# Agent attention and a mixture of experts on one core: the score products of a unit kept together on the tensor engine, and the first keys taken two units at a time

## The chip, the cores and the metric

The kernel runs on one core of one Trainium2 chip, in one launch. The metric is device time in microseconds (us). A core has five engines with an instruction queue each: PE (TensorE, matrix products; PEld are its weight loads), DVE (VectorE), ACT (ScalarE), POOL (GpSimd) and SP (SyncE, which here issues the loads). PE writes to PSUM, eight banks, from which DVE and ACT fetch. An f32 product shows as two records in the trace, an f16 product as one.

## The reference, cut to what matters

There are 4 batches of 11456 rows of 128 numbers (q, k, v), 49 agents, and 8 experts with a hidden layer of 1024.

```python
def sm(a, b):                       # softmax of scaled products
    s = scale * (a @ b.transpose(0, 2, 1))
    e = np.exp(s - s.max(-1, keepdims=True))
    return e / (e.sum(-1, keepdims=True) + 1e-09)

agent_v = sm(agents, k) @ v         # weighted values of each agent
x = sm(q, agents) @ agent_v         # every query's row
# expert per row: argmax of the cosine of x with 8 embeddings, and its gate
h = np.maximum(x[mask] @ w1[e], 0.0)
out[mask] = gate_w[mask, None] * (h @ w2[e])
```

All is f32. Rows of one batch go mostly to one expert; the few others ("strays") are answered apart.

## The kernel before, in words

A batch is cut into 12 units: 11 of 8 columns of 128 rows, and a small one of 2 columns of 96. For a unit of keys or of queries, `pe_T` (L412) turns the rows on PE, eight transposes into two PSUM banks (L419), and two copies bring them to SBUF: the first half on ACT (L424), the second on DVE (L422), or on ACT too where `two` is false. Then `scores` (L427) makes the products with the 49 agents (L432). Each product there takes 64 columns of the array: a column of 128 rows is two products, for the two halves of the array, and a whole unit is 16 products, 32 records. `k1_f32` (L435) does this for keys and keeps the scores and a running maximum; `q_unit` (L885) does it for queries and goes on to the softmax, to `rtp` (L935, the routing products) and to the rows `tt` that the expert's products read. In batches 2 and 3 every other unit of keys goes through `k1_pairs` (L456) instead, in f16 with DMA transposes. `k2_unit` (L503) takes the exponentials of the keys' scores and makes the weighted values (L523), again with half of the array: 8 products, 16 records a unit. The expert's products (`ffn_mm1` L1192, L1193; `ffn_mm2` L1216 to L1230) and the products that show which rows the shortcut holds for (`proved`, L1045, L1048) use the whole array.

Every unit is a Python generator. `run_step` lets all live generators go on by turns, and the order in which they write their instructions down is the program's order. Tile's scheduler then orders each engine's queue: of the instructions whose inputs and buffers are ready it puts the one that stands first in the program; inside `tc.high_priority(n)` an instruction counts as if it stood n instructions earlier, and `tc.issue_after(i)` (here `in_place` and `behind`) puts it behind instruction i on its engine. The first-layer products of the expert are asked for with 200. SP's queue is kept in the order of the program.

The program has two parts. `first` (L1493) takes batch 0's keys and values, the first four units of queries, and six units of batch 1's keys. From the point where `ffn_at[0]` is set, a loop over ticks runs the expert's products of the batches one after the other, and beside them the later keys, values and queries.

Buffers that matter: three for turned data (`xT`, XB = 3), four PSUM banks for transposes and first-layer products (`ps_h`), two for the expert's results (`ps_y`), and two for scores, weighted values, routing and the small products (`ps_s`). Ten buffers hold loaded units (LB = 10); a load waits until the tenth unit before it is used up. The weights of a batch's expert are loaded by `load_expert` (L872, L873), once `pick_expert` has found it from the weighted values.

Of the kernel before, what the change touches and what calls it, by code (L numbers as in the profile page):

```python
# [29 lines left out]
def kernel(ctx: ExitStack, tc: tile.TileContext, q, k, v, agents, emb, tau, w1, w2, out):  # L30
    nc = tc.nc
    pe, dve, act, pool, sp = nc.tensor, nc.vector, nc.scalar, nc.gpsimd, nc.sync

    B, N, C = q.shape
    A = agents.shape[1]
# [19 lines left out]
    LO = 64  # L55
    FP = 2 * P
    RW = E + 1 + A
    W = D + 1
    UT = 2
    UJ = UT * TJ  # L60
    NU = (J + UJ - 1) // UJ + 1
# [27 lines left out]
    def pss(name):  # L89
        return ps_s.tile([P, 512], F32, name=name, tag="s")  # L90
# [35 lines left out]
    ffn_at = [None]  # L126
# [3 lines left out]
    def used(*unit):  # L130

        ring[slot[unit]][1] = now[0]
# [40 lines left out]
    ident = cst.tile([P, P], F32, name="ident")  # L173
# [205 lines left out]
    def in_place(last):  # L379

        return tc.issue_after(last[-1].ins) if last else nullcontext()
# [23 lines left out]
    def run_max(kb, spv, p, n):  # L405
# [3 lines left out]
        else:  # L409
            dve.tensor_tensor(out=mr, in0=spv, in1=mr, op=ALU.max)  # L410

    def pe_T(src, p, n, two=True):  # L412

        xT = wk.tile([P, 2 * UJ, P], F16, name="fT", tag="xT", bufs=XB).rearrange("k c p -> k (c p)").bitcast(F32)
        for c0 in range(0, n, TJ):
            m = min(TJ, n - c0)
            tp = psh("fTp")
            for c in range(m):
                pe.transpose(out=tp[:, c * p : (c + 1) * p], in_=src[:p, c0 + c, :], identity=ident[:p, :p])  # L419
            dst = xT[:, c0 * p : (c0 + m) * p]  # L420
            if c0 and two:
                dve.tensor_copy(dst, tp[:, : m * p])  # L422
            else:
                act.copy(dst, tp[:, : m * p])  # L424
        return xT

    def scores(s, xT, b, p, n):  # L427

        for c in range(n):
            for h in range(0, p, LO):  # L430
                w = min(LO, p - h)
                pe.matmul(out=s[h : h + w, c * A : (c + 1) * A], lhsT=xT[:, c * p + h : c * p + h + w], rhs=aT_all[:, b, :],  # L432
                          start=True, stop=True, skip_group_check=True)

    def k1_f32(b, u):  # L435

        kb = blk_of(b, u)
        p, n = ushape(u)
        yield from here(("k", b, u))
        i = yield from take(x_slots)  # L440
        kb.at[u] = yield from take(s_slots)
        with in_place(warmed) if b + u == 0 else behind(asked["k", b, u]):
            kT = pe_T(units["k", b, u], p, n, b != 1 or u >= NEXT)
        used("k", b, u)
        yield 2
        s = pss("sp")
        scores(s, kT, b, p, n)
        give(x_slots, i)
        st = wk.tile([P, UJ, A], F32, name="s_u", tag="s_u", bufs=NU)[:p, :n]
        spv = s[:p, : n * A].rearrange("p (c a) -> p c a", a=A)  # L450
        act.copy(st, spv)
        run_max(kb, spv, p, n)
        kb.s[u] = st
        kb.k1 += 1
# [48 lines left out]
    def k2_unit(b, u, eng, g):  # L503

        kb = blk_of(b, u)
        p, n = ushape(u)
        while ("v", b, u) not in units:
            yield 1
        src = units["v", b, u]

        i = yield from take(d_slots)
        de = kds[i % len(kds)].rearrange("p c a -> p (c a)")
        d = de[:p, : n * A].rearrange("p (c a) -> p c a", a=A)
        eng.tensor_tensor(out=d, in0=kb.s[u], in1=kb.m[:p].unsqueeze(1).broadcast_to([p, n, A]), op=ALU.subtract)
        give(s_slots, kb.at[u])
        yield g[0]
        act.activation(d, d, AF.Exp, scale=SCALE)
        yield g[1]
        avp = pss("avp")

        for c in range(n):
            hs = slice(LO * (c % 2), LO * (c % 2) + LO)
            pe.matmul(out=avp[hs, :W], lhsT=de[:p, c * A : c * A + LO], rhs=src[:p, c, :], start=(c < 2), stop=(c >= n - 2),  # L523
                      skip_group_check=True)
        used("v", b, u)
        give(d_slots, i)
        if kb.k2 == 0:
            kb.x = sm.tile([P, W], F32, name="avx", tag="avx", bufs=2)
            dve.tensor_copy(kb.x, avp[:, :W])
        else:  # L530
            dve.tensor_tensor(out=kb.x, in0=avp[:, :W], in1=kb.x, op=ALU.add)
        kb.k2 += 1
# [352 lines left out]
    def q_unit(b, u, g):  # L885
        bt = batches[b]
        p, n = ushape(u)
        yield from here(("q", b, u))
        tt_of[b, u] = yield from take(t_slots, len(checks(b, u)) + sum(unit_of(t)[0] == u for t in range(NT)))
        f32 = b == 0 and u < LEAD  # L890
        i = yield from take(x_slots)
        with in_place(p_last) if p_last else behind(asked["q", b, u]):
            xT = pe_T(units["q", b, u], p, n, b < B - 1)
        used("q", b, u)
        yield g[0]
        s = pss("sp")
        scores(s, xT, b, p, n)
        give(x_slots, i)
        spv = s[:p, : n * A].rearrange("p (c a) -> p c a", a=A)
        mx = sm.tile([P, UJ], F32, name="qmx", tag="qmx")[:p, :n]  # L900
        dve.tensor_reduce(out=mx, in_=spv, axis=AX.X, op=ALU.max)
        ie = yield from take(qe_slots)
        e = wk.tile([P, UJ, A], F32, name="qe", tag="qe", bufs=LEAD)[:p, :n]
        dve.tensor_tensor(out=e, in0=spv, in1=mx.unsqueeze(2).broadcast_to([p, n, A]), op=ALU.subtract)
        yield g[1]
        act.activation(e, e, AF.Exp, scale=SCALE)  # L906
        yield g[2]
        i = yield from take(e_slots)
        e2 = e16[i % len(e16)]
        hi = e2[:p, :n, :A]  # L910
        i_ = act.copy(hi, e)  # L911
        if not ffn_at[0]:
            q_last[:] = [i_]
        (dve if f32 else pool).tensor_tensor(out=e2[:p, :n, LO : LO + A], in0=e, in1=hi, op=ALU.subtract)  # L914
        tt = wk.tile([P, UJ * P], F16, name="tt", tag="tt", bufs=TB)
        if f32:
            tp = psh("tp").bitcast(F16)
            for c in range(n):
                pe.transpose(out=tp[:, c * p : (c + 1) * p], in_=e2[:p, c, :], identity=ident16[:p, :p])
            act.copy(tt[:, : n * p], tp[:, : n * p])  # L920
        else:
            if ffn_at[0]:
                yield 8
            sp.dma_start_transpose(out=tt[:, : n * p].rearrange("k (c p) -> k c p", p=p),
                                   in_=e2[:p, :n, :].rearrange("p c k -> p (c k)"))
        give(e_slots, i)
        yield g[3]
        tts[b, u] = tt
        while not hasattr(bt, "r_hi"):
            yield 1  # L930
        s = (pss if ffn_at[0] else psh)("rtp")
        with in_place(y_last):
            for c in range(n):
                o = s[:p, c * RW : (c + 1) * RW]
                pe.matmul(out=o, lhsT=tt[:, c * p : (c + 1) * p], rhs=bt.r_hi, start=True, stop=False)  # L935
                pe.matmul(out=o, lhsT=tt[:, c * p : (c + 1) * p], rhs=bt.r_lo, start=False, stop=True)
        gi = group_of[u]
        us = groups[gi]
        if (b, gi) not in rtgs:
            rtgs[b, gi] = wk.tile([P, GC, E + 1], F32, name="rtg", tag="rtg", bufs=4)  # L940
        if not hasattr(bt, "qq"):
            bt.qq = sm.tile([P, 2, NCOL], F32, name="qq", tag="qq")
        rtg, qq = rtgs[b, gi], bt.qq
        c0 = ucol(u) - ucol(us[0])
        cs = slice(c0, c0 + n)
        if p < P:
            pmem(rtg[p:, cs], 1.0)
            pmem(qq[p:, :, ucol(u) : ucol(u) + n], 1.0)
        sv = s[:p, : n * RW].rearrange("p (c w) -> p c w", w=RW)
        rt = wk.tile([P, 2, UJ, A], F32, name="rt", tag="rt", bufs=1)[:p, :, :n]  # L950
        act.copy(rtg[:p, cs], sv[:, :, : E + 1])
        pool.tensor_tensor(out=rt[:, 1], in0=e, in1=e, op=ALU.mult)  # L952
        dve.tensor_tensor(out=rt[:, 0], in0=sv[:, :, E + 1 :], in1=e, op=ALU.mult)  # L953
        give(qe_slots, ie)
        yield 1
        pool.tensor_tensor(out=rt[:, :, :, : A // 2], in0=rt[:, :, :, : A // 2], in1=rt[:, :, :, A // 2 + 1 :], op=ALU.add)  # L956
        yield g[4]
        dve.tensor_reduce(out=qq[:p, :, ucol(u) : ucol(u) + n], in_=rt[:, :, :, : A // 2 + 1], axis=AX.X, op=ALU.add)
        routed[b, gi] = routed.get((b, gi), 0) + 1
        if routed[b, gi] == len(us):  # L960
            spawn(route_group(b, gi, sum(ushape(x)[1] for x in us)), 1, half=True)
# [750 lines left out]
```

## Time and profile before

| | |
|---|---|
| median of 3 runs | 716.54 us (716.29 to 717.41) |
| profiled execution | 717.31 us, span 715.4 us |
| PE busy | 660.7 us (92%) |
| DVE busy | 539.6 us (75%) |
| ACT busy | 459.8 us (64%) |
| POOL busy | 343.8 us (48%) |
| scores L432, PE | 98.7 us busy in 2496 records |
| mean granted clock of TensorE | 0.979 |

PE is the fullest engine. The groups' mean durations are latencies: products overlap, so what one costs PE is read from the starts of it and of the next. The page's slices show PE at nine or ten tenths nearly everywhere, with less near the start and at the very end.

### The profile page before, as it was taken

What the parts mean: (1) busy time and instruction counts of PE and PEld (TensorE: products, weight loads), DVE (VectorE), ACT (ScalarE), POOL (GpSimd) and SP (SyncE); (2) the same over time, 40 slices, a digit from 0 to 9 for tenths busy, and PEclk for the clock granted to TensorE, in tenths of its full rate; (3) what the DMA queues carried; (4) which work ended last, traced back from release to release, by engine and by line L of the source; (5) the groups of instructions that cost most, each with busy time, mean ns of one, the idle gap of its engine ahead of it and who ended that gap; (6) DMA issues with size and microseconds to landing.
All of it is one profiled execution on the core that took longest, in us unless ns stands there. A gap on an engine that the chain in (4) does not pass through costs nothing. (4 is left out here: it accounts for less than half of the span.)

```text
span 715.4 us, 23225 instructions
## 1 busy us (share of the span) xinstructions
PE 660.7 (92%) x9279; PEld 559.4 (78%) x9279; DVE 539.6 (75%) x1475; ACT 459.8 (64%) x1129; POOL 343.8 (48%) x579
## 2 busy tenths in 40 slices
PE   9987899999999899799999899999999898889996
PEld 7885777888888677678888787778888686777876
DVE  5768866787667998865767789975657699986983
ACT  4438646668678746666679854855577844976632
POOL 6004311395416555656524673764544663886500
PEclk9998899999999999999999999999999999999999
DMA  8995328699778349987969165994567242325232
GB/s 340 280 346 191 90 65 205 161 219 276 187 175 220 102 96 211 288 230 186 245 166 233 52 166 116 272 261 107 184 180 189 60 110 64 78 47 152 71 131 78
DMA packets 152823, 122.11 MB, mean 171 GB/s; under 512 B 72563, under 2 KB 128967, under 8 KB 152715
## 3 DMA queue, kind: packets, MB, share of 16 engines
q1 hardware_dynamic: 139275, 96.92, 52.9%
q10 hardware_dynamic: 13120, 23.47, 9.8%
q8 instruction: 73, 1.20, 0.7%
q0 software_dynamic: 320, 0.24, 0.1%
q14 instruction: 35, 0.29, 0.1%
HBM read 80.26 MB, written 23.79 MB: 145 GB/s over the span
## 5 line engine op out<-in xcount | busy, mean ns | idle before, releaser
L1054 ACT ACTIVATE vp<-vp 128x512 f32<-128x512 f32 x180 | 106.1, 589 | 18.7 <-PE vp L1045 15.8
L1201 ACT ACTIVATE hh<-hp 128x512 f16<-128x512 f32 (+1 forms) x124 | 72.9, 592 | 53.0 <-PE hp L1193 32.4
L1202 DVE SCALAR_TENSOR_TENSOR hh<-hp,hh 128x512 f16<-128x512 f32 (+1 forms) x124 | 84.0, 678 | 28.0 <-ACT hh L1201 27.4
L432 PE MATMUL sp<-aT_all,fT 128*64 128x49 f32 x2496 | 98.7, 225 | 3.6 <-DVE esa L1012 2.8
L432 PEld LDWEIGHTS sp<-aT_all,fT 128*64 128x64 f32 x2496 | 84.7, 137 | 21.8 <-issue 10.6
L1228 PE MATMUL yp<-w2p,hh 128*128 128x128 f16 (+1 forms) x492 | 92.6, 220 | 3.0 <-DVE w2p L842 2.3
L1229 PE MATMUL yp<-w2p,hh 128*128 128x128 f16 (+1 forms) x492 | 92.7, 220 | 0.0
L1230 PE MATMUL yp<-w2p,hh 128*128 128x128 f16 (+1 forms) x492 | 91.8, 220 | 0.0
L1045 PE MATMUL vp<-vm,tt 128*128 128x256 f16 x360 | 71.0, 274 | 3.1 <-DVE vmin L1051 1.4
L1192 PE MATMUL hp<-tt,gh 128*128 128x512 f16 (+1 forms) x184 | 69.3, 377 | 4.0 <-DVE fT L422 1.6
L424 ACT COPY fT<-fTp 128x512 f32<-128x512 f32 (+1 forms) x101 | 55.6, 564 | 24.7 <-PE fTp L419 16.8
L1244 DVE TENSOR_TENSOR ot<-yp,gs 128x512 f32<-128x512 f32 (+1 forms) x92 | 61.1, 670 | 12.0 <-PE yp L1230 5.9
L1193 PE MATMUL hp<-tt,gl 128*128 128x512 f16 (+1 forms) x184 | 69.0, 375 | 0.0
L995 POOL TENSOR_TENSOR nrm<-qq,half 128x16 f32<-128x16 f32 (+2 forms) x28 | 68.5, 2447 | 0.3
L914 POOL TENSOR_TENSOR e<-qe,e 128x392 f16<-128x392 f32 (+1 forms) x44 | 40.2, 914 | 56.9 <-ACT e L911 55.7
L1216 PE MATMUL yp<-lin,tt 128*128 128x128 f16 x720 | 63.6, 220 | 3.5 <-DVE ot L1244 3.5
L1225 PE MATMUL yp<-w2f,hh 128*128 128x128 f32 (+1 forms) x456 | 65.6, 281 | 0.0
L956 POOL TENSOR_TENSOR rt<-rt 128x384 f32<-128x384 f32 (+1 forms) x48 | 42.4, 884 | 44.7 <-DVE rt L953 26.3
L1225 PEld LDWEIGHTS yp<-w2f,hh 128*128 128x128 f32 (+1 forms) x456 | 58.4, 193 | 2.2
L1216 PEld LDWEIGHTS <-tt 128*128 128x128 f16 x720 | 49.8, 99 | 12.0 <-issue 4.5
L419 PE MATMUL fTp<-ident,qt 128*128 128x128 f32 x360 | 55.4, 281 | 2.5 <-DVE fT L422 1.1
L952 POOL TENSOR_TENSOR rt<-qe 128x392 f32<-128x392 f32 (+1 forms) x48 | 38.9, 810 | 37.2 <-ACT qe L906 24.4
(374 smaller groups left out, 1744.3 us busy)
## 6 DMA issues: line engine op xcount, KB each, us to landing
kt<-in_k_dram SPq DMA_DIRECT2D x44, 512.0 KB, 6.3
vt<-in_v_dram SPq DMA_DIRECT2D x44, 512.0 KB, 6.2
qt<-in_q_dram SPq DMA_DIRECT2D x44, 512.0 KB, 5.4
out_dram<-ot ACTq DMA_DIRECT2D x88, 256.0 KB, 3.3
w1s<-in_moe_w_dram SPq DMA_DIRECT2D x9, 512.0 KB, 3.8
w2s<-in_moe_w_dram SPq DMA_DIRECT2D x9, 512.0 KB, 5.9
tt<-e SPq DMA_TRANSPOSE x44, 3.9
kt<-in_k_dram SPq DMA_DIRECT2D x4, 96.0 KB, 3.8
```

Of the source, the lines that this page charges most:

```text
L432: pe.matmul(out=s[h : h + w, c * A : (c + 1) * A], lhsT=xT[:, c * p + h : c * p + h + w], rhs=aT_all[:, b, :], start=True, stop=True, skip ...
L1045: pe.matmul(out=z[:p, i * FP : (i + 1) * FP], lhsT=tt[:, c * p : (c + 1) * p], rhs=bt.vm[:, LO:], start=True, stop=True)
L1054: act.activation(z[:p], z[:p], AF.Relu, scale=-1.0, accum_out=bt.vsum[:p, at : at + 1])
L1192: pe.matmul(out=hp[:, :m], lhsT=bt.gh[:, fs], rhs=tt, start=True, stop=False)
L1193: pe.matmul(out=hp[:, :m], lhsT=bt.gl[:, fs], rhs=tt, start=False, stop=True)
L1201: h_last[:] = [act.activation(hh[:, :m], hp[:, :m], AF.Relu)]
L1202: dve.scalar_tensor_tensor(out=hl[:, :m], in0=hp[:, :m], scalar=0.0, in1=hh[:, :m], op0=ALU.max, op1=ALU.subtract)
L1216: pe.matmul(out=yp[:p, c, :], lhsT=tc_, rhs=bt.lin[:, h], start=(c == 0 and h == 0), stop=False, skip_group_check=True)
L1225: y_last[:] = [pe.matmul(out=y, lhsT=hh[:, cs], rhs=bt.w2f[:, f], start=False, stop=last, skip_group_check=True)]
L1228: pe.matmul(out=y, lhsT=hh[:, cs], rhs=wh, start=False, stop=False, skip_group_check=True)
L1229: pe.matmul(out=y, lhsT=hh[:, cs], rhs=wl, start=False, stop=False, skip_group_check=True)
L1230: y_last[:] = [pe.matmul(out=y, lhsT=hl[:, cs], rhs=wh, start=False, stop=last, skip_group_check=True)]
```

## The change

Scores and weighted values that are written down after `ffn_at[0]` is set come into `tc.high_priority(300)`; before that point nothing changes for them, with one exception. For batch 0's keys, a unit of odd number (1, 3, 5, 7, 9) writes its scores only when the unit two further on has been turned, and puts them behind the last transpose of that unit on PE. `pe_T` notes its last transpose in `turn` for this.

```diff
+    turn, k_turned = [], {}
+    def whole():
+        return tc.high_priority(300) if ffn_at[0] else nullcontext()
...
     def pe_T(src, p, n, two=True):
...
-                pe.transpose(out=tp[:, c * p : (c + 1) * p], in_=src[:p, c0 + c, :], identity=ident[:p, :p])
+                turn[:] = [pe.transpose(out=tp[:, c * p : (c + 1) * p], in_=src[:p, c0 + c, :], identity=ident[:p, :p])]
...
     def k1_f32(b, u):
...
+        k_turned[b, u] = turn[0]
         yield 2
+        two = b == 0 and u % 2 and u + 2 < NU
+        while two and (b, u + 2) not in k_turned:
+            yield 1
         s = pss("sp")
-        scores(s, kT, b, p, n)
+        with in_place([k_turned[b, u + 2]]) if two else whole():
+            scores(s, kT, b, p, n)
...
     def k2_unit(b, u, eng, g):
...
-        for c in range(n):
-            hs = slice(LO * (c % 2), LO * (c % 2) + LO)
-            pe.matmul(out=avp[hs, :W], lhsT=de[:p, c * A : c * A + LO], rhs=src[:p, c, :], start=(c < 2), stop=(c >= n - 2),
-                      skip_group_check=True)
+        with whole():
+            for c in range(n):
+                hs = slice(LO * (c % 2), LO * (c % 2) + LO)
+                pe.matmul(out=avp[hs, :W], lhsT=de[:p, c * A : c * A + LO], rhs=src[:p, c, :], start=(c < 2), stop=(c >= n - 2),
+                          skip_group_check=True)
...
     def q_unit(b, u, g):
...
-        scores(s, xT, b, p, n)
+        with whole():
+            scores(s, xT, b, p, n)
```

## Rows read from the trace of the kernel before

**Rows 1.** Windows: length, busy us of each engine, then PEclk, DMA share, GB/s
```profile
8.00:29.00 21.00, 21.00 (x397) 18.66 (x395) 13.32 (x25) 10.04 (x21) 6.15 (x33) 1.00 1.08 341
...
44.00:53.00 9.00, 6.98 (x78) 6.74 (x78) 5.04 (x21) 2.08 (x6) 0.00 (x0) 0.81 0.92 344
...
103.00:650.00 547.00, 513.51 (x7257) 434.57 (x7256) 419.92 (x1125) 374.16 (x940) 296.03 (x464) 0.99 0.66 168
```

**Rows 2.** Timeline of PE: start us, length us, line, operation, tiles, count
```profile
355.12 0.38 PE L1192 MATMUL hp<-tt,gh 128*128 128x512 f16 x1
355.33 0.38 PE L1193 MATMUL hp<-tt,gl 128*128 128x512 f16 x1
355.64 1.14 PE L432 MATMUL sp<-aT_all,fT 128*64 128x49 f32 x32
356.71 0.28 PE L1045 MATMUL vp<-vm,tt 128*128 128x256 f16 x1
```

**Rows 3.** Timeline of PE, two units of scores in one run
```profile
231.85 2.07 PE L432 MATMUL sp<-aT_all,fT 128*64 128x49 f32 x64
233.86 0.39 PE L1045 MATMUL vp<-vm,tt 128*128 128x256 f16 x2
```

**Rows 4.** Timeline of PE, 114 to 123 us, scores in ten runs
```profile
114.26 0.56 PE L432 MATMUL sp<-aT_all,fT 128*64 128x49 f32 x12
114.75 0.39 PE L1045 MATMUL vp<-vm,tt 128*128 128x256 f16 x2
115.07 0.32 PE L432 MATMUL sp<-aT_all,fT 128*64 128x49 f32 x2
115.32 0.66 PE L419 MATMUL fTp<-ident,kt 128*128 128x128 f32 x4
...
121.69 1.13 PE L432 MATMUL sp<-aT_all,fT 128*64 128x49 f32 x30
122.75 1.09 PE L419 MATMUL fTp<-ident,kt 128*128 128x128 f32 x8
```

**Rows 5.** Timeline of PE, other units in several runs, the first and the last
```profile
107.05 0.67 PE L432 MATMUL sp<-aT_all,fT 128*64 128x49 f32 x16
...
150.75 0.44 PE L523 MATMUL avp<-vt,kd 128*64 128x129 f32 x4
...
537.70 0.32 PE L432 MATMUL sp<-aT_all,fT 128*64 128x49 f32 x2
...
538.49 1.13 PE L432 MATMUL sp<-aT_all,fT 128*64 128x49 f32 x30
```

**Rows 6.** Timeline of ACT and DVE, copies of turned halves, two units
```profile
107.52 0.57 ACT L424 COPY fT<-fTp 128x512 f32<-128x512 f32 x1
...
108.35 0.69 DVE L422 COPY fT<-fTp 128x512 f32<-128x512 f32 x1 [1.59 <-PE fTp L419]
...
550.31 0.61 ACT L424 COPY fT<-fTp 128x512 f32<-128x512 f32 x1
...
551.69 0.57 ACT L424 COPY fT<-fTp 128x512 f32<-128x512 f32 x1
```

**Rows 7.** Groups by line: busy us, mean ns, idle us before and its releasers
```profile
L432 PE MATMUL sp<-aT_all,fT 128*64 128x49 f32 x2496 | 98.7, 225 | 3.6 <-DVE esa L1012 2.8 <-DVE w2p L842 0.5 <-ACT kd L517 0.3
...
L935 PE MATMUL rtp<-r_hi,tt 128*128 128x58 f16 x352 | 25.9, 190 | 5.1 <-DMA tt<-e 3.0 <-DVE w2p L842 0.9 <-DVE ee L1401 0.6
```

**Rows 8.** Timeline of PE, first keys and first products on the expert's weights
```profile
8.92 1.09 PE L419 MATMUL fTp<-ident,kt 128*128 128x128 f32 x8
9.94 1.14 PE L432 MATMUL sp<-aT_all,fT 128*64 128x49 f32 x32
...
52.82 1.96 PE L698 MATMUL gp<-avT,w1s 128*128 128x49 f32 x16 [0.45 <-DVE qmx L901]
```

**Rows 9.** Landing of two k loads issued 41.1 and 42.0, then w1s issued 48.7
```profile
DMA to landing us min/median/max: 9.0/9.1/9.3
...
DMA to landing us min/median/max: 4.0/4.0/4.0
```

## The prediction

> **What bounds the kernel now.** I read the windows of equal work first, then PE's timeline, then the copies that feed the products, then the landings of the loads. In the long stretch in which the expert's products run, 103 to 650 us, PE is busy 513.5 of 547 us (94%), at the full granted clock (0.99, the 2.4 GHz level) [rows 1]. DVE has 420 and ACT 374 of the same 547. So 94% of a PE microsecond saved there is a microsecond of the end, as long as PE's input is ready. Before 53 us it is otherwise: PE is full from 8 to 29 us, but the DMA engines are full as well (share 1.08, and 0.92 from 44 to 53, where PE is at 0.81) [rows 1].
>
> **The price that the change is after.** Scores (L432) and weighted values (L523) use the array as two halves of 64 columns; all other products use it whole. PE's timeline shows what each change between the two costs. The product L1193 takes 0.21 us to its successor when that is an ordinary one (355.12 to 355.33 is the same form), but the scores behind it start 0.31 later: 0.09 to go in [rows 2]. A whole unit of scores (32 records, two to a product) lasts 1.07 us to the next product [rows 2], two units back to back 2.01 [rows 3]: 0.94 for 32 more, 0.0294 each, so 1.07 holds 0.94 of work and 0.13 to come out. One break inside a unit costs 0.09 + 0.13, with rounding 0.23 us. Checked on a part: 12 records should take 0.13 + 0.35 = 0.48, and take 0.49 (114.26 to 114.75); 2 records should take 0.19 and take 0.25, since the cut goes through a pair of halves [rows 4].
>
> The Trainium skill, "TensorEngine Tiling (Array Packing)", section "Key Properties", says that a change of tiling mode drains TensorE, and "TensorE: Matmul & The Clock Gate", section "Single matmul latency", puts the fixed part of a single product at 166 ns at the full clock; two drains would make a break 0.33 us (an estimate from that page), and the 18 breaks below 6.0 us instead of 5.0. The 0.23 of this trace decides.
>
> **How many breaks there are.** From 114.26 to 122.75 three units of scores lie in ten runs, of 12, 2, 8, 20, 2, 10, 2, 8, 2 and 30 records, with transposes and vp, hp and yp products between them (the first two and the last run in [rows 4]). Start to next start the ten runs take 4.48 us, where three whole units take 3.21; with seven further entries at 0.094 that is 1.93 us for seven breaks, 0.28 each. In the whole stretch I count 18 breaks in 12 units: two at 107, these seven, one each at 325, 372, 465 and 537, two at 484, and three in weighted values, which are cut at 150, 180 and 183 us (first and last in [rows 5]). 18 x 0.28 = 5.0 us. A cut at 92 us is in a unit that is written down before the new priority holds, and stays.
>
> **What the priority removes.** A scores or weighted-values product of this stretch is placed as if it stood 300 instructions earlier, ahead of the first-layer products at 200. What cuts the units now is ready work that stands earlier in the program, so all 18 can go: 5.0 x 0.94 = 4.7 us.
>
> **What it adds.** Three things, none shown by this trace.
> (a) The scores no longer queue behind older work, so they come when their first half is ready. A unit's transposed data comes by two copies. In 33 of its 55 whole units the second ends over 0.6 us after the first, more than the 0.56 that half a unit takes (0.09 + 0.47); the first and the last of the 33 are in [rows 6] (0.57 after 107.52, then 0.69 after 108.35; 550.92, then 552.26). Now the scores usually start 1 to 4 us after both, and this lag is hidden. If they start at once, PE, which has other work ready, puts it between the halves: a new break of 0.23. Bounds: none, and 33 x 0.23 x 0.94 = 7.2 us. The row nearest to this is the crowded stretch at 105 to 128 us, where six units follow their copies within about 1 us: one of them has a first run of 16 records, exactly half [rows 5]. One in six of 62 units is 10: 10 x 0.23 x 0.94 = 2.2 us.
> (b) With no slack behind its copy, a unit can make PE itself wait, and everything behind it in PE's queue waits too (yp and hp, then ACT and DVE). Scores idle PE for 3.6 us over 84 units now; rtp products, which do come close behind their input, idle it for 5.1 over 44 [rows 7]. At rtp's 0.116 a unit against 0.043 it would be 62 x 0.073 = 4.5 us; without rtp's waits for a DMA (3.0), which scores don't have, 0.3. I take 0.3; below nothing is possible by up to 1, if earlier scores shorten rtp's own waits.
> (c) Nine pairs of units now share one entry and one exit by chance ([rows 3] is one). Priority can part them (9 x 0.23 = 2.1 us at worst) or make as many new ones. I take 0.
>
> **First keys two at a time.** From 8 us on transposes and scores alternate, unit by unit, with no idle PE [rows 1, 8]. Five pairs of units now share a change: 5 x 0.23 = 1.2 us of PE. The transposes that are moved ahead need the next load 2 us earlier at most once (the fourth unit, at 9.9), and the buffers of the turned data just suffice, three for three. What is late next is the first expert: its weights are issued at 48.7 us and land 4.0 us later, and the products on them start at 52.82 [rows 8, 9]. The k loads ahead of them on SP's queue were issued at 41.1 and 42.0 and needed 9.0 and 9.3 us, so they land at 50.1 and 51.3 [rows 9], and 0.5 MB at the 344 GB/s of these microseconds [rows 1] takes 1.5 us: the weights land right behind them however early they are asked for. So I cost the saving at 0, hidden by the DMA stream; the other bound is the whole 1.2 us, if the weights kept their 4.0 us and came earlier.
>
> The Trainium skill, "DMA: Bandwidth & Descriptors", section "Queues, rings and completion order", says that each DMA engine takes the descriptors of one ring in order. By that the weights can't pass the keys and the gain is 0; without it, 1.2 us. The spacing of the landings here agrees with the rule.
>
> **Sum.** -4.7 + 2.2 + 0.3 + 0 = -2.2 us. The profiled execution took 717.31 us (715.4 of span and 1.9 around it), so 715.1 for it; the median of the runs shown is 0.77 lower, and 716.54 - 2.2 = 714.3 is the forecast. About 0.2% of this time, 1.4 us, can be told from no change.
>
> **Rivals.**
> Torn at the halves (slower). The mechanism is (a) alone: every one of the 33 units with a late second copy is cut there. 7.2 + 0.3 - 4.7 = +2.8: 719.3 us. It decides from about 22 units on (4.7 / 0.217), where it eats the whole gain. For it: the lag is there in 33 of 55 units. Against: a unit also needs a score bank, of which there are two, and while it waits for one its second half lands.
> A draw. Some 18 to 22 units are cut at the half, about as many breaks as go: 716.5 us. For it: the same rows; this is only the middle of (a).
> All of it. No new cuts, and the first keys' 1.2 us come through: -4.7 - 1.2 = -5.9, 710.6 us. For it: PE is the bound for 547 us. Against: rows 6 and 9.
> It doesn't do what it says. What cuts the units is that their input isn't ready, not older work; then priority changes only the weighted values (3 x 0.25 x 0.94 = 0.7): 715.8 us. Against: the cuts at 114 to 122 fall after 12, 2 and 8 records, not at halves.
>
> **How the numbers follow.** Forecast 0.36, of which 0.27 is beyond 1.4 us and 0.09 within; its own range is 712.5 to 716. All of it 0.17, faster. A draw 0.20, of which 0.18 same and 0.02 slower. Torn 0.21, slower. Doesn't do it 0.06, same. Together faster 0.44, same 0.33, slower 0.23. The range 710.8 to 719.3 leaves out half of "all of it" and less than half of "torn".
>
> **What would show it.** In PE's timeline, the runs of L432's line of under 32 records: with the change, cuts after 2, 8, 10 or 12 records should be gone, and what is left should be 16 and 16. Ten units cut so bears out the forecast, over 22 the slower rival, none the best case. Weighted values should all be runs of 16 or 32. The idle time before the scores should stay under 5 us. Scores of the first keys should show as runs of 64, and the first products on the expert's weights should still start at 52.5 to 53 us; if they start near 51.6, the DMA was not the cover I take it for. The prediction is wrong if PE's idle time in 103 to 650 us moves by more than 3 us, since then the order of the work, and not the price of the breaks, sets the result.

## The result, and the profile after

The changed kernel takes 709.96 us (median of 6 runs, 708.62 to 713.9), the kernel before 717.93 beside it (6 runs). The ratio is 0.9898, 95% interval 0.9874 to 0.9922: 8.0 us less, where 2.2 less was forecast. 709.96 lies below the range (710.8 to 719.3). The profiled execution of the changed kernel, from which all its rows come, is the longest of its six: 713.9 us, span 711.9, so its rows show 3.4 of the 8.0 us. The ratios here leave out slow runs (over 1.5% above the fastest of their kernel: two, of the changed kernel at 190), and are not quotients of the medians shown, from which they differ by up to 0.5%.

Lines are numbered anew: scores are L438 now, transposes L425, weighted values L535, the expert's products L1205 to L1243. In the kernels of the experiments they shift by a few more; the tile names stay.

The windows of the changed kernel, with two short ones added (columns as in [rows 1]):

```profile
8.00:29.00 21.00, 20.95 (x430) 19.47 (x429) 14.41 (x26) 11.33 (x24) 6.25 (x34) 1.00 1.08 341
44.00:53.00 9.00, 6.08 (x72) 5.81 (x71) 5.35 (x20) 2.74 (x8) 0.14 (x1) 0.81 1.00 360
103.00:650.00 547.00, 521.97 (x7409) 447.17 (x7407) 420.71 (x1145) 378.20 (x963) 301.22 (x480) 0.98 0.68 172
160.00:166.00 6.00, 4.08 (x66) 3.29 (x65) 3.29 (x7) 2.69 (x6) 5.83 (x10) 1.00 1.12 237
167.00:173.00 6.00, 5.41 (x41) 4.40 (x42) 2.79 (x6) 2.34 (x6) 0.48 (x2) 0.50 0.85 238
```

From 103 to 650 us PE does 7409 products where it did 7257 [rows 1]. Its idle time there is 547 less 521.97, 25.0 us; it was 33.5. The prediction had said that it is wrong if this moves by more than 3 us. At the same time the clock is worse: from 160 to 166 us it is full, from 167 to 173 at 0.50, the 1.2 GHz level.

PE's timeline of the changed kernel: the first keys, the first products on the expert's weights, a stretch that answers to [rows 4], and a long wait:

```profile
9.02 1.97 PE L425 MATMUL fTp<-ident,kt 128*128 128x128 f32 x16
10.92 2.07 PE L438 MATMUL sp<-aT_all,fT 128*64 128x49 f32 x64
12.92 1.97 PE L425 MATMUL fTp<-ident,kt 128*128 128x128 f32 x16
...
53.70 1.70 PE L710 MATMUL gp<-avT,w1s 128*128 128x49 f32 x7 [2.29 <-DMA w1s<-in_moe_w_dram]
...
109.69 0.67 PE L438 MATMUL sp<-aT_all,fT 128*64 128x49 f32 x16
110.29 0.66 PE L425 MATMUL fTp<-ident,kt 128*128 128x128 f32 x4
110.88 0.67 PE L438 MATMUL sp<-aT_all,fT 128*64 128x49 f32 x16
...
163.40 0.67 PE L438 MATMUL sp<-aT_all,fT 128*64 128x49 f32 x16
167.59 1.01 PE L1229 MATMUL yp<-lin,tt 128*128 128x128 f16 x8 [3.51 <-DVE ot L1257]
```

The first keys are as built: 64 records of scores behind 16 transposes, 3.90 us for two units. The cuts after 2, 8, 10 and 12 records [rows 4] are gone. Six units of scores are still cut, every one 16 and 16, as at 109.69 and 110.88; weighted values are never cut. In the whole program the half-array products lie in 112 runs, 134 before.

What the scores wait for, and the two groups that changed most:

```profile
L438 PE MATMUL sp<-aT_all,fT 128*64 128x49 f32 x2496 | 97.8, 226 | 3.9 <-DVE esa L1025 2.6 <-DVE m_run L410 0.7 <-DVE rt L966 0.6
...
L1229 PE MATMUL yp<-lin,tt 128*128 128x128 f16 x720 | 64.1, 223 | 10.7 <-DVE ot L1257 10.7
...
L948 PE MATMUL rtp<-r_hi,tt 128*128 128x58 f16 x360 | 28.6, 192 | 4.5 <-DMA tt<-e 3.9 <-DVE qe L917 0.5
```

Scores idle PE for 3.9 us (3.6 in [rows 7]). The new waits are elsewhere: yp waits 10.7 us for DVE to empty its bank, 3.5 before. In the kernel before PE's longest waits were (us in all, times, longest):

```profile
PE tp L919 <- DVE e L914: 4.8, 2, 3.3
PE yp L1216 <- DVE ot L1244: 3.5, 4, 1.4
PE sqT L1286 <- DMA xq<-in_q_dram,ix: 3.2, 2, 1.8
```

The longest wait of yp in the changed kernel, in the timeline of all engines:

```profile
165.96 0.23 POOL L1029 TENSOR_TENSOR el<-el,la 128x16 f32<-128x16 f32 x1
...
166.22 0.25 DVE L1032 RECIPROCAL gs<-el 128x16 f32<-128x16 f32 x1 [0.85 <-POOL el L1029]
...
166.50 0.31 ACT L1036 ACTIVATE gs<-gs,iall 128x16 f32<-128x16 f32 x1
...
166.84 1.29 DVE L1257 TENSOR_TENSOR ot<-yp,gs 128x512 f32<-128x512 f32 x2 [0.38 <-ACT gs L1036]
```

The gate of the rows comes from POOL by way of DVE and ACT, and only then does DVE take the result out of its bank. POOL is busy for 5.83 of the 6 us from 160 on. PE stands still for 3.51 us, and from 166.3 us, still inside this wait, the clock is at the 1.2 GHz level for 6.8 us.

**An account of a span.** For the comparisons below each profile's span is split in three: *idle* (no product is running), *clock* (half of the busy time at the 1.2 GHz level) and *work* (the rest). Before: 54.7 + 11.4 + 649.3 = 715.4. After: 50.1 + 21.5 + 640.2 = 711.9 (rounded). Waits too short to show between overlapping products count as work. Each split is of one profiled execution; the times and ratios are of all runs.

### The profile page after: what moved, and what is told of

The parts are those of the page before. It is cut to its first block, busy times and chain, and to the rows that moved or that the text cites. A ratio compares the mean times of both kernels' runs of the same rounds, so it can differ in the third digit from the quotient of the medians.

```text
span 711.9 us, 23232 instructions
## 1 busy us (share of the span) xinstructions
PE 661.7 (93%) x9279; PEld 567.1 (80%) x9279; DVE 533.3 (75%) x1475; ACT 456.5 (64%) x1129; POOL 340.9 (48%) x579
## 4 chain that ended last, share of the span: by engine, by line
PE 67%; DVE 18%; ACT 5%; DMA 4%; issue 3%; POOL 2%; ACTq 0%; POOLq 0%; SPq 0%; DVEq 0%
PE sp L438 9%; PE fTp L425 8%; PE avp L535 6%; PE yp L1229 5%; PE yp L1238 4%; PE hp L1205 4%; PE vp L1058 4%; PE hp L1206 4%; PE yp L1241 3%; PE yp L1243 3%; PE yp L1242 3%; DVE hh L1215 2%; DVE sel L791 2%; DVE ot L1257 2%; PE gp L710 1%
## 5 line engine op out<-in xcount | busy, mean ns | idle before, releaser
L438 PE MATMUL sp<-aT_all,fT 128*64 128x49 f32 x2496 | 97.8, 226 | 3.9 <-DVE esa L1025 2.6
L438 PEld LDWEIGHTS sp<-aT_all,fT 128*64 128x64 f32 x2496 | 85.8, 139 | 17.3 <-issue 4.3
L1241 PE MATMUL yp<-w2p,hh 128*128 128x128 f16 (+1 forms) x492 | 95.8, 224 | 0.2 <-DVE w2p L854 0.2
L1242 PE MATMUL yp<-w2p,hh 128*128 128x128 f16 (+1 forms) x492 | 95.3, 224 | 0.0
L1243 PE MATMUL yp<-w2p,hh 128*128 128x128 f16 (+1 forms) x492 | 94.0, 224 | 0.0
L1229 PE MATMUL yp<-lin,tt 128*128 128x128 f16 x720 | 64.1, 223 | 10.7 <-DVE ot L1257 10.7
L1205 PE MATMUL hp<-tt,gh 128*128 128x512 f16 (+1 forms) x184 | 69.4, 378 | 2.7 <-DVE hh L1215 1.8
L1238 PE MATMUL yp<-w2f,hh 128*128 128x128 f32 (+1 forms) x456 | 62.9, 278 | 0.0
L1238 PEld LDWEIGHTS yp<-w2f,hh 128*128 128x128 f32 (+1 forms) x456 | 56.6, 190 | 2.0
L969 POOL TENSOR_TENSOR rt<-rt 128x384 f32<-128x384 f32 (+1 forms) x48 | 40.0, 832 | 37.4 <-DVE rt L966 34.2
L425 PE MATMUL fTp<-ident,qt 128*128 128x128 f32 x360 | 55.0, 279 | 1.2 <-ACT vp L1067 1.0
L1241 PEld LDWEIGHTS <-hh 128*128 128x128 f16 (+1 forms) x492 | 49.9, 101 | 5.3 <-issue 0.5
```

The lines of the kernel that those rows point to most:

```text
L425: turn[:] = [pe.transpose(out=tp[:, c * p : (c + 1) * p], in_=src[:p, c0 + c, :], identity=ident[:p, :p])]
L1205: pe.matmul(out=hp[:, :m], lhsT=bt.gh[:, fs], rhs=tt, start=True, stop=False)
L1229: pe.matmul(out=yp[:p, c, :], lhsT=tc_, rhs=bt.lin[:, h], start=(c == 0 and h == 0), stop=False, skip_group_check=True)
L1238: y_last[:] = [pe.matmul(out=y, lhsT=hh[:, cs], rhs=bt.w2f[:, f], start=False, stop=last, skip_group_check=True)]
L1241: pe.matmul(out=y, lhsT=hh[:, cs], rhs=wh, start=False, stop=False, skip_group_check=True)
L1242: pe.matmul(out=y, lhsT=hh[:, cs], rhs=wl, start=False, stop=False, skip_group_check=True)
```

## The experiments

Three theories go through most of the runs. B: breaks alone set the time. S (first called E): an earlier start of the scores is worth something of its own. L: PE's waits and the clock are set anew by each order of PE's queue, whatever the breaks. P, Q and W are for single runs; M and D, for the last four, are told there. A time is the median; "before" is the kernel before, run beside it.

### The two parts alone

first keys alone (in `whole`), and priority alone (in `k1_f32`):
```diff
-        return tc.high_priority(300) if ffn_at[0] else nullcontext()
+        return nullcontext()
```
```diff
-        two = b == 0 and u % 2 and u + 2 < NU
+        two = False
```

> Only the first keys two units at a time; no new priority. PE changes between half and whole array in 129 runs of half-array products instead of 134 (five pairs of units merged). Theory P (the prediction: the 1.2 us saved on PE end behind the DMA stream, the first products on the expert's weights still start at 52.5 to 53 us): no change, 0 to -0.4 us. Rival Q (the saving is carried through, PE sets the pace of the start): -1.2 us or more, those products at about 51.6 us. A third case: the gap that the saving opens lowers the granted clock, and the time rises by 1 us or more.

> Only the priority of scores and weighted values; first keys as before. 117 runs instead of 134, all of it after 103 us. Theory B (a break costs 0.23 to 0.28 us of PE and nothing else changes): 17 x 0.28 x 0.94 = -4.5 us. Rival E (the measured -8 us comes mostly from something else that priority does, such as scores that come earlier and what follows them): -6 to -8 us. If the first keys carry a part, this kernel has less than the whole change by that part.

First keys alone: 718.32 us against 717.74, ratio 0.9999 (0.9979 to 1.0019), as P has it. Priority alone: 710.75, 0.9896 (0.9875 to 0.9918), the same as the whole change: 7.5 us less, where B wanted 4.5 and E 6 to 8. So the gain is the priority's, and more than its breaks. PE's timeline of the first keys alone shows where its 1.6 us less of work (647.7) go:

```profile
51.33 0.22 PE L438 MATMUL sp<-aT_all,fT 128*64 128x49 f32 x1
52.92 2.20 PE L710 MATMUL gp<-avT,w1s 128*128 128x49 f32 x16 [1.37 <-DMA w1s<-in_moe_w_dram]
```

The products on the expert's weights start at 52.92, as before (52.82), behind 1.37 us of waiting for the DMA.

### Fewer breaks by other means

Two kernels keep each unit together in other ways. In "kept" (without the first keys' part) a unit's first product keeps its old place, and only the rest follow it closely. In "untorn" (the whole change) scores begin with the second half, so that they can't start before both halves have landed.

```diff
# kept, in scores; weighted values alike
+                with (whole() if head else nullcontext()), (in_place(head) if ffn_at[0] else nullcontext()):
                     i = pe.matmul(...)
+                head = head or [i]
# untorn
-        for c in range(n):
+        for c in [*range(TJ, n), *range(min(TJ, n))]:
...
+                with (in_place(head) if ffn_at[0] else nullcontext()):
```

> The breaks without the earlier start: the first product of each unit of scores or weighted values stands where it stood before, the other products of the unit are queued behind it at priority 300. First keys as before. 118 runs instead of 134. Theory B: the same as the priority alone, -16 x 0.28 x 0.94 = -4.2 us. Rival E (the earlier start is what pays): well under half of what the priority alone gives, 0 to -2 us.

> The whole change, and a unit's scores begin with the half that is copied last, the other products queued behind the first: no unit can be torn at its half. 106 runs instead of the 112 of the whole change. Theory B: six breaks fewer than the whole change, 6 x 0.23 = 1.4 us faster than it, about -9.4 us against before. Rival W (scores that wait for their second copy make PE's queue wait or start later): no faster than the whole change, or slower by up to 2 us.

Kept: 118 runs, 721.4 us, 1.0048 (1.0029 to 1.0067). Untorn: 106 runs, the fewest of all, 724.47 us, 1.0096 (1.007 to 1.0122). Both do less work than before (643.3 and 640.7 against 649.3) and both are slower. Idle and clock together are 77.2 and 77.9 us, 66.1 before. B alone falls. E and W miss too: kept was to gain 0 to 2 us by E, and untorn was to lose at most 2 on the whole change by W; it lost over 14. PE's longest waits in the untorn kernel:

```profile
PE sqT L1302 <- DMA xq<-in_q_dram,ix: 5.5, 2, 3.1
PE tp L935 <- DVE e L930: 4.5, 2, 3.3
PE hp L1208 <- DVE hh L1218: 4.3, 4, 1.7
PE sp L440 <- DVE esa L1028: 3.3, 1, 3.3
...
PE yp L1232 <- DVE ot L1260: 2.6, 2, 2.4
```

Only one of them stands before scores, and it was there before (2.8 us; tp had 4.8). What grew is a gather for the strays (sqT, 3.2 before) and the first layer's wait for its own buffers (hp, 1.3 before).

### Other strengths of the priority

```diff
-        return tc.high_priority(300) if ffn_at[0] else nullcontext()
+        return tc.high_priority(220) if ffn_at[0] else nullcontext()   # the other kernel: 100
```

> The whole change with the priority of scores and weighted values at 220 instead of 300. 113 runs of half-array products, as good as the 112 of the change, but another order of all products in the long stretch. Theory L (a change of these products is worth its PE work, and beside that every new order of PE's queue gains or loses up to some 5 us of idle time and low clock, by chance of which product stands before a result that is late): work 8 to 9 us below before, the time anywhere from -10 to +2 us, and not the same as the change's -8. Rival S (300 saves idle time for a reason of its own, earlier scores): within 2 us of the whole change, -6 to -10 us.

> The whole change with that priority at 100, below the first-layer products' 200. 113 runs, another order again; scores come a little later than at 300. Theory L: work 8 to 9 us below before, the time anywhere from -10 to +2 us. Rival S: between the kernel that keeps the earlier start (-7.4) and the one that starts scores where they stood (+3.5), so -2 to -5 us.

At 220: 728.18 us, 1.0139 (1.0099 to 1.0178), beside 719.4 for the kernel before. At 100: 714.09, 0.994 (0.99 to 0.9981). Each has 113 runs, and work 641.3 and 640.4, as with 300. Idle and clock are 83.8 and 71.7. S as put is out, though the time at 100 lies within its -2 to -5: 220 is above the first-layer products' 200, as 300 is, and loses 8.8 us where S wanted a gain of 6 to 10. L has the work right, but its range (-10 to +2) is too narrow for 220 as well. PE's longest waits at 220:

```profile
PE yp L1229 <- DVE ot L1257: 7.4, 3, 4.7
PE tp L932 <- DVE e L927: 4.7, 2, 3.2
PE sqT L1299 <- DMA xq<-in_q_dram,ix: 3.3, 2, 1.9
PE hp L1205 <- DVE hh L1215: 3.2, 3, 1.7
```

The changed kernel has the second of them (4.5), of the last 1.8, for sqT 0.2, and for yp more in all (10.7). The one wait of 4.7 for DVE's result is longer than any of its own.

### The order changed without the change

```diff
-                    with tc.high_priority(200):
+                    with tc.high_priority(240):   # the other kernel: 170
```

This is the first-layer products' priority, in the kernel before.

> The kernel before, with the priority of the first-layer products at 240 instead of 200; scores and weighted values at none. 131 runs of half-array products instead of 134. Theory L: a new order with hardly less work (-1 us), the time off by up to 5 us either way. Rival S: nothing that it names is touched, so -1 us by the three breaks, and no more than 1 us beside it.

> The kernel before, with the priority of the first-layer products at 170 instead of 200. 130 runs of half-array products instead of 134. Theory L: work 1 to 1.5 us less, the time off by up to 5 us either way, and not by the same as with 240. Rival S: -1.3 us by the four breaks, and no more than 1 us beside it.

At 240: 724.28 us, 1.0074 (1.0042 to 1.0105). At 170: 715.12, 0.9936 (0.9907 to 0.9964). Runs are 131 and 130, work 647.2 and 647.3. So 4.9 us more and 4.3 us less come with hardly a break removed, where S allowed 1 us beside the breaks. L's up to 5 us is about what came, and a single comparison of two orders can be off by that much either way.

### The price of a break, measured

Priority alone, with one product more per unit of scores (128x1, f16, whole array; its result is not used): in the middle of each unit ("cut"), or behind it ("beside"). In both, the products of a unit are also queued one behind the other.

```diff
+            if c == n // 2 and ffn_at[0]:        # beside: once, behind the loop
+                with in_place(at):
+                    at = [pe.matmul(out=s[:, 500:501], lhsT=ident16, rhs=ident16[:, :1], ...)]
```

> The priority of the change without the first keys' part, and in each of the 62 units of scores of the long stretch one extra product on the whole array (128x1, f16), queued in the middle of the unit: every unit is cut once on purpose. To be compared with the next kernel, which has the same product behind each unit, where the array changes anyway. Theory B's price (0.23 us a break, from the rows): PE's work 62 x 0.23 = 14 us above the next kernel. If a break costs more than the rows of scores show (transposes behind scores are slower too), up to 0.4 us each, 25 us above.

> The same 62 extra products, each queued behind its whole unit of scores, where the array changes in any case. PE's work is expected 62 x 0.03 to 0.1 = 2 to 6 us above the kernel with the priority alone (641.4), and 14 (or up to 25) us below the kernel that is cut in the middle. Its time may lie off by some us either way by the new order.

Cut: 172 runs, 730.0 us, 1.0166 (1.0108 to 1.0225). Beside: 126 runs, 731.23, 1.0183 (1.0126 to 1.0241). There are two runs of each. The times can't be told apart, since the second has 11.0 us more idle time (61.7 and 50.7). The rows can. PE's timeline of the cut kernel:

```profile
133.24 0.67 PE L443 MATMUL sp<-aT_all,fT 128*64 128x49 f32 x16
133.84 0.18 PE L439 MATMUL sp<-ident 128*128 128x1 f16 x1
133.95 0.67 PE L443 MATMUL sp<-aT_all,fT 128*64 128x49 f32 x16
134.55 0.39 PE L1214 MATMUL hp<-tt,gh 128*128 128x512 f16 x1
```

A cut unit lasts 1.31 us to the next product, a whole one 1.07 [rows 2]: a break costs 0.24, the small product with it. Over the span, work is 653.8 against 641.4 with the priority alone: 12.4 us for 55 more runs and 62 products, 0.23 for each run if the products cost nothing. Against the kernel beside it is 7.4 for 46 runs, 0.16, where 14 had been expected from 62. So the predicted 0.23 is borne out by the row, and by the whole span it is 0.16 to 0.23.

### The change at other orders

First-layer products at 170 and 240 with the whole change:

> The whole change, with the priority of the first-layer products at 170 instead of 200, the setting with which the kernel before was 4 us faster. 114 runs of half-array products. Theory L (idle time and low clock go by the chance of the order): work 640 to 641 us again, the time anywhere from -10 to +5 us against before, not the sum of the two gains. If the two gains add up, -12 us.

> The whole change, with the priority of the first-layer products at 240, the setting with which the kernel before was 5 us slower. 117 runs. Theory L: work 641 to 642 us, the time anywhere from -10 to +5 us against before. If the two effects add up, -3 us.

At 170: 708.07 us, 0.9862 (0.9826 to 0.9897), 114 runs. At 240: 712.28, 0.9916 (0.9886 to 0.9947), 117 runs. That the two gains add up is not excluded at 170 (7.4 to 12.5 us less, 12 by the sum), and excluded at 240 (3.8 to 8.2 less, 3 by the sum). The change was ahead of the kernel before with the same setting at three orders, by different amounts. What was open: is it worth 8 us whatever the order (M), or its breaks alone, with the luck of the order on top (D)? Two more pairs, at 190 and 150:

> The kernel before, its first-layer products asked for with 190 instead of 200: 131 runs of half-array products, 134 before. By the theory that PE's waits are drawn anew with each order: work within 2 us of before (649), time anywhere from -5 to +8 us against before. By the theory that breaks alone set the time: -0.6 us (3 runs of 0.2). It is one half of a pair with the whole change at 190.

> The whole change, first-layer products asked for with 190: 112 runs of half-array products, as many as with 200. At 170, 200 and 240 the change took 5, 8 and 11.5 us off the kernel before of the same setting (each by the ratios to before). Theory M, the change is worth some 8 us whatever the order, because it takes 5 us of breaks and some 3 of short waits off PE's own work: 5 to 11 us below the kernel before at 190. Theory D, only the breaks' 4 to 5 us are the change's and the rest was the luck of three orders: a pair may come out anywhere from -13 to +4, and the two new pairs together nearer to -4 than to -8.

> The kernel before, first-layer products asked for with 150: 130 runs of half-array products. Work within 2 us of before; time anywhere from -6 to +8 us against before by the theory of the order, -0.8 us by that of the breaks alone.

> The whole change, first-layer products asked for with 150: 112 runs of half-array products. Theory M: 5 to 11 us below the kernel before at 150. Theory D: anywhere from -13 to +4, nearer to -4 with the pair at 190 taken in. In both, work (the span less PE's idle time and the clock's loss) is 639 to 642 us.

At 190: 716.03 us without the change, 0.9982 (0.9957 to 1.0006), and 715.16 with it, 0.9931 (0.9893 to 0.9969). At 150: 728.31 without, 1.0122 (1.0089 to 1.0154), and 708.33 with it, 0.9823 (0.9771 to 0.9875). The five pairs, in us, the gain from the two ratios at 717.5 (at 170 and 240 the two kernels of a pair did not run beside each other):

| first layer at | work without, with | idle + clock without, with | gain |
|---|---|---|---|
| 150 | 646.5, 641.4 | 79.9, 67.6 | 21.5 |
| 170 | 647.3, 641.5 | 68.4, 64.1 | 5.3 |
| 190 | 648.9, 643.5 | 63.9, 70.1 | 3.7 |
| 200 | 649.3, 640.2 | 66.1, 71.6 | 7.3 |
| 240 | 647.2, 641.1 | 75.5, 70.3 | 11.3 |

Neither theory stands as put. M wanted every pair between 5 and 11: one pair has 21.5, and that at 190 lies below (its two intervals overlap). D wanted the new pairs near 4 on average: they have 12.6. What holds in all five is the work: 5.1 to 9.1 us less with the change, 6.3 in the mean, and the two columns don't overlap (one kernel, at 190, came out 1.5 above the 639 to 642 expected). Idle and clock move by -12.3 to +6.2, -2.0 in the mean, which five pairs don't tell from nothing. PE's longest waits without the change at 150:

```profile
PE tp L919 <- DVE e L914: 4.9, 2, 3.3
PE rtp L935 <- DMA tt<-e: 4.0, 1, 4.0
PE rtp L935 <- DVE qe L904: 3.5, 5, 1.2
PE yp L1216 <- DVE ot L1244: 3.5, 4, 1.7
```

The changed kernel with 170 (708.07 us) and with 150 (708.33) are the best versions run. They did not run beside the changed kernel with 200; its interval overlaps that of 170, and that of 150 touches it.

## Why the prediction was wrong, step by step

**The bound.** Right: PE sets the time in the long stretch. But less work on PE shows in the end only after what its waits and its clock do.

**The price of a break.** Right, if a little high over the span: 0.23 forecast, 0.24 (with a small product) read from a row made for it, 0.16 to 0.23 from the work of whole spans.

**What the priority removes (-4.7).** Right: the 18 cuts that it counted are gone. An estimate of what all steps from and to half-array products cost over their plain step, from 103 us on, is 23.9 us, 28.9 before (each step from one start to the next, against the usual step of its form). What is taken as usual and what is done with idle time move the difference between 3.6 and 5.0.

**(a) New tears (+2.2) and (c) shared changes (0).** This step failed in size. Six units are cut, at the halves as predicted, not ten. And (c), costed at 0, brought more units into one run: 14 times a unit follows another directly, 9 before. So from 103 us on there are 17 fewer runs (90, 107 before: 18 cuts gone, 6 new, 5 more shared), where the sum had 8. The 3.6 to 5.0 us just named are net of all this; the sum had 2.5. In most of the 55 whole units the second copy still ends over 0.6 us after the first; that a lag of the copies makes a tear was the error. The prediction read that scores start 1 to 4 us after both copies and would now start at once. With copies and scores matched in order, they started 11.2 us after on average before, and 7.6 us with the change; 13 of 55 start within 1 us or earlier, and the unit at 109.69 is cut though its second half lands only 0.34 us after its first. "Torn at the halves" is out by the same count, 6 where it needed 22.

**(b) Stalls behind copies (+0.3).** The term for the scores is right (3.6 to 3.9 us); what it stands for is not, and this is the step that failed in its mechanism. I costed the wait of the unit that moves and took every other wait, and the clock, as it was. The idle time in the stretch fell by 8.5 us and the clock's loss rose: from the first to the last hp product idle, clock and work are 36.9, 4.8 and 567.4 before, 28.6, 11.8 and 560.4 after. Over the span idle and clock are +5.5 in the profiled execution, and by the medians, which differ by 8.0 where work differs by 9.1, about +1, if work is the same in every execution. That small sum is one case: over the other kernels with the priority, the two with added products left out, it is -2.0 (first layer at 170) to +17.7 (at 220) against before. The bounds put on (b), -1 and +4.5, were far too narrow for that, and the range with them.

**First keys (0).** Right: 0.9999 alone, with the DMA as the cover. In the whole change gp starts at 53.70, though, later than the 52.5 to 53 named. Its weights were issued 0.9 us earlier than before (47.8 us) and landed 0.9 later, at 53.6, and PE waits 2.29 us for them. With the priority alone gp starts at 53.7 too, but for another reason: there the weights land at 52.8, and gp stands behind scores without a wait. The first hp product of the whole change is 3.2 us later (93.8 and 90.6); why is open.

**The rivals.** "All of it" (710.6) came nearest in the number, with a wrong half: the first keys' 1.2 us don't come through. Of its other half, no new cuts (4.7 us), the net of 3.6 to 5.0 us is close, though six cuts came.

**What is left open.** Of the 9.1 us of work, 3.6 to 5.0 are breaks and up to 1.6 the first keys; the other 2 to 4, for which the sum had no term, have no place yet. That they are short waits between products is not shown. The other four pairs, with 14 to 19 fewer runs for 22, have 5.1 to 6.1 us less work, so this part may belong to one order. Why one order has its 3 to 5 us waits and another not is read from each trace afterwards, not explained; that it is chance is not shown either.

## What to carry to other kernels

A change to the priority of one group of instructions orders the whole queue anew. Cost the work that it saves from the rows, but give the waits a width from a control: shift another priority a little in the kernel before, and see how far the time goes with little work saved (here from -0.6% to +1.2%). Judge such a change by pairs at several orders, not by one, with the work and the waits read apart.

## What the runs showed of the hardware

Low clock mostly came with long waits of PE. In the changed kernel the 1.2 GHz level holds from 53.7 us for 13.7 us, behind the wait of 2.29 us, and from 166.3 for 6.8, during the wait of 3.51 and after it; the products L1241 to L1243 follow at 0.11 us there and at 0.056 at the full clock. The link is not strict: in the untorn kernel a wait of 3.09 us before sqT, up to 304.7 us, was followed by 10 us at the full clock:

```profile
304.69 0.30 PE L1302 MATMUL sqT<-ident,xq 128*128 128x128 f32 x1 [3.09 <-DMA xq<-in_q_dram,ix]
...
304.70:315.00 10.30, 10.30 (x172) 8.78 (x173) 7.49 (x23) 7.87 (x21) 6.98 (x13) 1.00 1.11 299
```

The longest such stretch of a kernel took 6.8 us (before) to 13.7, and the clock's loss over the span went from 11.4 us before to 24.0 (priority 220). From 167 to 173 us alone, PE's 5.41 busy us at half the clock are 2.7 lost, beside the 3.51 of the wait.
